# Earlier loads of x for batches 2 and 3, pooling ten chunks sooner, seven more softmax denominators on GpSimd, and a new order of the work

## The chip, the cores and the metric

The kernel runs on one core of a Trainium2 chip. Its metric is the device time of one execution in microseconds (us); lower is better. Nothing is exchanged with another core. Five engines work side by side and each runs its own list of instructions in the order in which the program put them: TensorE (PE in the profile, with PEld for its weight loads), VectorE (DVE), ScalarE (ACT), GpSimd (POOL) and SyncE (SP, which here only issues DMAs). An instruction that waits on a semaphore holds everything behind it on its engine.

## The reference

Two parts follow each other: an attention block with a few learned queries, and a feed-forward layer that takes the larger of two linear maps.

```python
B, N, m, C = 4, 12544, 32, 128
h = mab(I, x)            # 32 inducing points attend to all 12,544 rows of a batch ("pooling")
y = mab(x, h)            # each row attends to the 32 rows of h

def mab(q, kv):
    a = exp(scale * q @ kv.T - max);  a /= a.sum(-1) + 1e-09
    return a @ kv

h1, h2 = y @ w1, y @ w2                  # 128 -> 1024
out = maximum(h1, h2) @ w_out            # 1024 -> 128
```

Input and output are float32, 50,176 rows of 128 (25.7 MB each way).

## The kernel before, in words

A batch has 98 chunks of 128 rows. The maximum of two linear maps is computed as `h1 + relu(h2 - h1)`, and since every row of y is a mixture of the 32 rows of h, both maps are applied to h once for a batch (`hwd` for the difference w2 - w1, `m1` for w1 with w_out), so that the big matmuls contract over 32 values only. A chunk then passes these steps:

- **Scores** (`stage`, L596, L610; exp on ScalarE, L629): x transposed times h, four quarters of a block side by side in columns of the PE array ("column" mode). The result e2 (before division by its sum) is kept in six buffers.
- **Phases** (`phase`, L1011, matmuls L1069): four contractions over 32 rows run side by side in the four row groups of the array ("row" mode). Results go through relu to SBUF, by ScalarE (L1085) or VectorE (L1088).
- **Finals** (`final_one`, L864, L876): relu times w_out over eight pieces of 128, in the whole array ("full" mode).
- **Eviction** (`evict_group`, L893, L907): VectorE multiplies a group (mostly four chunks) by the reciprocal of the denominators and SP stores it (L935), from six output buffers.

The 28 blocks (7 a batch; blocks 0 to 6 are batch 0, 7 to 13 batch 1, 14 to 20 batch 2, 21 to 27 batch 3; block 20 is one chunk wide, most are four) have 108 groups.

The denominators of e2 come in one of two ways. `dens` (L656) has PE multiply e2 by ones (L671, one matmul for each chunk of width), VectorE takes the reciprocal from PSUM (L681). For a block marked `turned` (L594) SP transposes e2 by DMA (`den_turn`, L684, L688), GpSimd adds 32 values by halving in five additions (`den_sum`, L692, L698 and L700), and VectorE takes the reciprocal from SBUF (`den_rp`, L704, L707).

Pooling of batches 1 to 3 runs during the batch before: SP transposes x by DMA in 14 pieces (`transpose_x_dma`, L168, L172; batches alternate between two buffers), PE makes scores of 16 chunks at a time (`pool_scores`, L323, L329, six units), ScalarE the exp (L340), SP transposes it (`pool_turn`, L364, L366), and PE sums two units at a time with x (`pool_accum`, L369, L385). The transposed exps of the pooling and of the denominators share five buffers (tag `eT`). x itself is loaded by GpSimd's queue (`load_x`, L160, L166) into 12 buffers, seven for a batch. A one-element copy (`pace`, L164) ahead of the first load of a batch makes GpSimd wait for the value it reads. In the kernel before, the loads of batches 2 and 3 wait for the last pooling sum of the batch ahead (L418).

Batch 0 is different: its x is loaded first, transposed on PE (L235), copied from PSUM by VectorE (L246) or ScalarE (L249) as the table `COPY` says, and scored and summed in the order written in the string `HEAD`.

After the head a planner at build time sets the order. It keeps a clock of its own (`ck`) and at each step chooses between a phase, a final, scores and side work; the table `DEV` overrides it at numbered steps. Side work is put on a list at a count of finished chunks (L1103 to L1123) and issued once `ready` (L1129) says so by that clock. Which instruction waits for which is found afterwards, from the data.

Of the kernel before, what the change touches and what calls it, by code (L numbers as in the profile page):

```python
# [102 lines left out]
def kernel(  # L103
# [10 lines left out]
    B, N, C = x.shape  # L114
# [6 lines left out]
    P1 = 14  # L121
# [75 lines left out]
    with tc.manual_schedule(engines={ET.PE, ET.DVE, ET.Activation, ET.Pool, ET.SP}):  # L197
# [26 lines left out]
        st = [dict() for _ in range(B)]  # L224
# [90 lines left out]
        NU = K // U  # L315
# [48 lines left out]
        def pool_turn(b, u):  # L364
            eT = etp.tile([128, 4, 128], F16, name=f"eT_{b}_{u}", tag="eT", bufs=NEU)
            nc.sync.dma_start_transpose(eT, st[b]["eu", u][0].rearrange("p (j t) -> p j t", j=4))  # L366
            st[b]["eT", u] = eT, ck.pe

        def pool_accum(b, u):  # L369
# [52 lines left out]
            if last and b + 1 < B:  # L422
                for i in range(7):
                    load_x(b + 1, i, acc[:, C : C + 1] if i == 0 else None)
# [168 lines left out]
        for n, blk in enumerate(blocks):  # L593
            blk.turned = n > 20  # L594
# [128 lines left out]
        for n in ("h", "e"):  # L723
# [4 lines left out]
            ((0, 8, "A"), (8, 6, "D")),  # L728
            ((0, 6, "A"), (6, 8, "D")),
            ((0, 8, "A"), (8, 6, "D")),  # L730
            ((0, 6, "A"), (6, 8, "D")),
            ((0, 6, "A"), (6, 1, "A")),
            ((0, 5, "D"), (5, 2, "D")),
            ((0, 3, "D"), (3, 4, "A")),
            ((0, 4, "A"), (4, 3, "A")),
            ((0, 4, "D"), (4, 3, "D")),
            ((0, 4, "D"),),
            ((0, 2, "A"), (2, 1, "D")),
# [6 lines left out]
            T0.0 T0.1 C0.1 I C0.0 L0 T1.0 A0.2 C1.0 T1.1 C1.1 S0 S1 X0 X1 L1 H0 T2.0 E0 T2.1 C2.1 T3.0 C2.0  # L745
            A1.2 T3.1 S2 C3.0 X2 T4.0 H1 C3.1 L2 T4.1 S3 T5.0 T5.1 C4.0 H2 X3 C4.1 S4 T6.0 E1 C5.0 H3 T6.1
            X4 C6.0 C6.1 H4 T7.0 C5.1 E2 T7.1 S5 C7.0 T8.1 T8.0 C8.0 C8.1 C7.1 X5 S7 X7 S6 T9.0 H5 C9.0
            T10.0 T10.1 E5 X6 C10.0 C10.1 S8 E6 H7 X8 E4 N0.0 S10 S9 H6 E3 X9 H8 H9 E8 E9 E7 X10 E10 H10 e h
            W0.1 s N1.0 D0.1 G0 Y0.1 G1 Y1 D1.0 D2.1 Y0.2 W1.0 P0 w P1
# [143 lines left out]
        def evict_group(g, end):  # L893
# [38 lines left out]
            for b, c, s, m in runs:  # L932
                h = 2 if m == 4 and (groups.index(g) in (56, 60, 64, 68, 72, 76) or 78 <= groups.index(g) < 95) else m
# [26 lines left out]
        def want_linear():  # L960
# [142 lines left out]
        for b in range(1, B):  # L1103
            base = DONE0[b - 1]
# [24 lines left out]
        def ready(f, a):  # L1129

            now = ck.pe
            if f is den_turn:
                return a[0].staged <= now
            if f is den_sum:
                return a[0].den[1] + 7.5 <= now
# [184 lines left out]
```

## Time and profile before

| | |
|---|---|
| median of 3 runs | 324.26 us (324.13 to 324.92) |
| the profiled execution's own time | 324.39 us |
| its span, first to last instruction | 322.5 us |
| PE, DVE, ACT, POOL busy | 98%, 87%, 87%, 12% |
| granted PE clock | 1.0 throughout |
| PE's first and last matmul start | 1.19 and 319.43 us |

How to read it: the page gives busy time by engine, the span in 40 slices (tenths), the chain of work that ended last, and groups of instructions by source line with count, total and mean. A matmul's own duration overlaps the next one's, so the cost of a matmul is read from the distance between starts, or from the chain. About 1.9 us of the time lie outside the span.

### The profile page before, as it was taken

Reading aid. Unit: us, or ns where it says so; the run is one execution under the profiler, and the core shown is the slowest. Engines: PE = TensorE matmul, PEld = TensorE weight load, DVE = VectorE, ACT = ScalarE, POOL = GpSimd, SP = SyncE. Lnnn points to the kernel's source line nnn. Section 1 sums busy time; section 2 is a strip of 40 time slices with the busy share of each in tenths; the row PEclk is TensorE's granted clock in tenths of the full one; section 3 lists DMA queues with packets and bytes.
Section 4 is the critical chain, followed back from the end, with each engine's and each line's share of the span. In section 5 each row is a group of like instructions: output and inputs, shape, how many; then the busy total and the mean of one; then the engine's idle time right before and its main releaser. Section 6 shows DMA issues by size and latency. Waiting matters only on the chain.

```text
span 322.5 us, 12605 instructions
## 1 busy us (share of the span) xinstructions
PE 315.6 (98%) x5375; PEld 239.8 (74%) x5375; DVE 281.4 (87%) x508; ACT 281.8 (87%) x561; POOL 37.8 (12%) x90
## 2 busy tenths in 40 slices
PE   7899999999999999999999999999999999999996
PEld 3776777777777777777777777777777777777786
DVE  3369999988989998999989989988998999899974
ACT  3779999998978999999898999998869999999960
POOL 7470000000040000000040000000006400302000
PEclk9999999999999999999999999999999999999999
DMA  8999999954279999794279999893424322324233
GB/s 205 207 268 213 218 249 203 210 136 133 100 150 245 221 254 216 181 194 139 99 151 242 218 258 207 160 211 120 118 96 103 135 80 100 109 100 128 87 118 116
DMA packets 77320, 53.99 MB, mean 167 GB/s; under 512 B 56112, under 2 KB 64976, under 8 KB 77264
## 3 DMA queue, kind: packets, MB, share of 16 engines
q1 hardware_dynamic: 71232, 39.42, 50.0%
q0 software_dynamic: 5888, 13.70, 21.7%
q8 instruction: 42, 0.69, 0.9%
q14 instruction: 14, 0.11, 0.1%
q10 hardware_dynamic: 144, 0.07, 0.1%
HBM read 27.28 MB, written 25.69 MB: 164 GB/s over the span
## 4 chain that ended last, share of the span: by engine, by line
PE 93%; DMA 5%; ACT 1%; issue 1%; POOL 0%; DVE 0%; POOLq 0%
PE ps L876 62%; PE ps L1069 22%; DMA xn<-in_x_dram 5%; PE ps L610 2%; PE ps L385 2%; PE ps L329 1%; PE ps L671 1%; PE ps L833 1%; ACT e L629 0%; PE ps L505 0%; ACT hwd L482 0%; PE ps L235 0%; PE ps L303 0%; PE ps L430 0%; PE ps L258 0%
## 5 line engine op out<-in xcount | busy, mean ns | idle before, releaser
L1085 ACT ACTIVATE relu<-ps 128x512 f16<-128x512 f32 x462 | 244.1, 604 | 23.0 <-PE ps L1069 15.0
L1088 DVE TENSOR_SCALAR relu<-ps 128x512 f16<-128x512 f32 x322 | 206.1, 682 | 16.2 <-PE ps L1069 14.8
L876 PE MATMUL ps<-woutp,relu 128*128 128x128 f16 x3136 | 216.9, 220 | 0.0
L876 PEld LDWEIGHTS <-relu 128*128 128x128 f16 x3136 | 176.6, 98 | 39.4 <-issue 28.9
L1069 PE MATMUL ps<-e,hwd 32*128 32x512 f16 (+2 forms) x888 | 88.2, 358 | 0.1
L907 DVE TENSOR_TENSOR o<-ps,rp 128x512 f32<-128x512 f32 (+3 forms) x80 | 51.2, 640 | 1.8 <-PE ps L876 1.3
L1069 PEld LDWEIGHTS <-hwd 32*128 32x128 f16 x888 | 24.5, 91 | 20.9 <-issue 0.8
L1069 PE MATMUL ps<-m,e 32*128 32x128 f16 x381 | 38.7, 217 | 0.0
L1069 PEld LDWEIGHTS <-e 32*128 32x128 f16 x381 | 21.2, 92 | 2.9 <-issue 0.4
L907 DVE TENSOR_TENSOR o<-ps,rpt 128x512 f32<-128x512 f32 (+3 forms) x28 | 17.3, 618 | 4.1 <-PE ps L853 2.2
L166 POOL DMA_DIRECT2D xn<-in_x_dram x33 | 17.8, 553 | 6.7 <-DMA xn<-in_x_dram 4.6
L164 POOL COPY pace<-hacc 128x1 f32<-128x1 f32 x2 | 0.4, 188 | 133.1 <-DVE hacc L418 133.1
L246 DVE COPY xT<-ps 128x768 f16<-128x768 f16 (+6 forms) x11 | 4.8, 458 | 8.9 <-PE ps L235 8.9
L340 ACT ACTIVATE eu<-ps 128x512 f16<-128x512 f32 x18 | 10.9, 614 | 0.1
L629 ACT ACTIVATE e<-ps 128x512 f16<-128x512 f32 (+2 forms) x21 | 10.4, 568 | 0.2 <-PE ps L610 0.2
L235 PE MATMUL ps<-identity,xn 128*128 128x128 f16 x98 | 8.1, 219 | 2.3 <-DMA xn<-in_x_dram 1.8
L535 POOL COPY m1bd<-m 32x128 f16<-32x128 f16 x4 | 1.1, 287 | 76.7 <-DVE m L530 76.6
L249 ACT COPY xT<-ps 128x768 f16<-128x768 f16 (+5 forms) x10 | 6.5, 671 | 3.0 <-PE ps L235 2.9
L698 POOL TENSOR_TENSOR w1T<-den 128x256 f32<-128x256 f16 (+1 forms) x7 | 4.4, 633 | 38.6 <-DMA den<-e 38.6
L700 POOL TENSOR_TENSOR w1T<-w1T 128x64 f32<-128x64 f32 (+4 forms) x28 | 8.4, 302 | 2.2
L235 PEld LDWEIGHTS <-xn 128*128 128x128 f16 x98 | 5.6, 97 | 4.0 <-DMA xn<-in_x_dram 2.2
L610 PE MATMUL ps<-xT,hT 128*32 128x512 f16 (+3 forms) x114 | 8.2, 361 | 0.0
(93 smaller groups left out, 117.0 us busy)
## 6 DMA issues: line engine op xcount, KB each, us to landing
out_dram<-o SPq DMA_DIRECT2D x68, 256.0 KB, 2.8
xn<-in_x_dram POOLq DMA_DIRECT2D x24, 448.0 KB, 10.1
out_dram<-o SPq DMA_DIRECT2D x54, 128.0 KB, 1.8
wf<-in_moe_w_dram POOLq DMA_DIRECT2D x4, 256.0 KB, 5.9
xn<-in_x_dram POOLq DMA_DIRECT2D x3, 224.0 KB, 8.8
xT<-xn SPq DMA_TRANSPOSE x42, 3.8
xf<-in_x_dram SPq DMA_DIRECT2D x1, 512.0 KB, 3.7
xf<-in_x_dram SPq DMA_DIRECT2D x1, 384.0 KB, 4.2
```

The source lines that it names most:

```text
L166: nc.gpsimd.dma_start(out=xn_at[b, i][lo:hi, 0:n, :], in_=xr[b, lo:hi, k0 : k0 + n, :])
L235: nc.tensor.transpose(ps[:, j, :], xn_at[0, i][:, g + j, :], identity16)
L249: nc.scalar.copy(out=dst, in_=ps[:, 0:m, :])
L340: nc.scalar.activation(out=eu, in_=ps, func=AF.Exp, scale=scale, accum_out=st[b]["es"][:, u : u + 1])
L610: nc.tensor.matmul(out=ps[32 * q : 32 * (q + 1), 128 * t : 128 * (t + n)], lhsT=hq, rhs=xT[:, c : c + n, :], start=True, stop=True, tile_p ...
L629: nc.scalar.activation(out=blk.e2[:, lo:hi], in_=ps[:, lo:hi], func=AF.Exp, scale=st[0]["rs"] if blk.b == 0 else scale,)
L700: nc.gpsimd.tensor_add(acc[:, :, 0:n], acc[:, :, 0:n], acc[:, :, n : 2 * n])
L876: nc.tensor.matmul(out=g.ps[:, 128 * c : 128 * (c + 1)], lhsT=g.blk.relu[q][:, 128 * (jb * w4 + t) : 128 * (jb * w4 + t + 1)], rhs=woutp[: ...
L907: nc.vector.tensor_mul(osb[:, 0:n, :], g.ps[:, 0 : n * C].rearrange("p (s c) -> p s c", s=n), rp)
L1069: nc.tensor.matmul(**seq[i])
L1085: nc.scalar.activation(out=dst, in_=src, func=AF.Relu)
L1088: nc.vector.tensor_scalar(out=dst, in0=src, scalar1=0.0, scalar2=None, op0=ALU.max)
```

## The change

- `load_x` of batches 2 and 3 moves from the end of `pool_accum` to the end of `pool_turn` of the last unit; the first load now waits for the last pooling exp of the batch ahead.
- Pooling of batches 2 and 3 (x transposes, scores, transposes of the exps, sums) is put on the list 10 chunks earlier.
- Blocks 9, 10, 11, 12, 16, 19 and 20 become `turned`: their denominators go by DMA transpose and GpSimd. Outside the last batch GpSimd's additions are released 4.0 us (not 7.5) after the transpose by the planner's clock.
- In the head, `COPY` hands other pieces to the other engine, and `HEAD` has a new order: among others the first cast of w1 by GpSimd stands ahead of the first load of batch 1's x, and the subtraction w2 - w1 is made in four pieces of 256 rather than two of 512.
- Seven groups (88 to 94) are no longer stored in halves.
- `DEV` is new from step 948 on.

```diff
@@ pool_turn
             st[b]["eT", u] = eT, ck.pe
+            if u == NU - 1 and b + 1 < B:
+                for i in range(7):
+                    load_x(b + 1, i, st[b]["eu", u][0][:, 0:1] if i == 0 else None)
@@ pool_accum
-            if last and b + 1 < B:
-                for i in range(7):
-                    load_x(b + 1, i, acc[:, C : C + 1] if i == 0 else None)
@@
-            blk.turned = n > 20
+            blk.turned = n > 18 or n in (9, 10, 11, 12, 16)
@@ COPY
-            ((0, 8, "A"), (8, 6, "D")),
+            ((0, 8, "D"), (8, 6, "A")),
             ((0, 6, "A"), (6, 8, "D")),
-            ((0, 8, "A"), (8, 6, "D")),
+            ((0, 7, "A"), (7, 7, "A")),
             ((0, 6, "A"), (6, 8, "D")),
-            ((0, 6, "A"), (6, 1, "A")),
-            ((0, 5, "D"), (5, 2, "D")),
-            ((0, 3, "D"), (3, 4, "A")),
-            ((0, 4, "A"), (4, 3, "A")),
-            ((0, 4, "D"), (4, 3, "D")),
+            ((0, 7, "D"),),
+            ((0, 7, "D"),),
+            ((0, 2, "D"), (2, 5, "A")),
+            ((0, 4, "D"), (4, 3, "A")),
+            ((0, 7, "D"),),
             ((0, 4, "D"),),
-            ((0, 2, "A"), (2, 1, "D")),
+            ((0, 2, "D"), (2, 1, "A")),
@@ HEAD (the last two lines of each)
-            T10.0 T10.1 E5 X6 C10.0 C10.1 S8 E6 H7 X8 E4 N0.0 S10 S9 H6 E3 X9 H8 H9 E8 E9 E7 X10 E10 H10 e h
-            W0.1 s N1.0 D0.1 G0 Y0.1 G1 Y1 D1.0 D2.1 Y0.2 W1.0 P0 w P1
+            H7 N3.0 E6 S9 E4 S10 E3 H8 X10 N2.0 X9 E8 H6 E10 E7 E9 e H9 H10 W0.1 h s D0.1 N5.0 N4.0 G0 G1
+            Y0.1 Y1 Y0.2 D1.0 D2.1 W1.0 P0 w P1
@@ evict_group
-                h = 2 if m == 4 and (groups.index(g) in (56, 60, 64, 68, 72, 76) or 78 <= groups.index(g) < 95) else m
+                h = 2 if m == 4 and (groups.index(g) in (56, 60, 64, 68, 72, 76) or 78 <= groups.index(g) < 88) else m
@@ DEV
...
@@ when side work is listed
-            base = DONE0[b - 1]
+            base = DONE0[b - 1] - (10 if b > 1 else 0)
@@ ready
             if f is den_turn:
-                return a[0].staged <= now
+                d = st[a[0].b + 1] if a[0].b < B - 1 else {}
+                quiet = a[0].b == B - 1 or a[0].index >= 7 or ("T", 13) in d and ("eT", NU - 1) in d
+                return a[0].staged <= now and quiet
             if f is den_sum:
-                return a[0].den[1] + 7.5 <= now
+                return a[0].den[1] + (7.5 if a[0].b == B - 1 else 4.0) <= now
```

More of the change, by code (lines that the diff above doesn't have):

```diff
@@ L727 @@
         COPY = (
-            ((0, 8, "A"), (8, 6, "D")),
+            ((0, 8, "D"), (8, 6, "A")),
             ((0, 6, "A"), (6, 8, "D")),
-            ((0, 8, "A"), (8, 6, "D")),
+            ((0, 7, "A"), (7, 7, "A")),
             ((0, 6, "A"), (6, 8, "D")),
-            ((0, 6, "A"), (6, 1, "A")),
-            ((0, 5, "D"), (5, 2, "D")),
-            ((0, 3, "D"), (3, 4, "A")),
-            ((0, 4, "A"), (4, 3, "A")),
-            ((0, 4, "D"), (4, 3, "D")),
+            ((0, 7, "D"),),
[3 more added lines that the diff above has]
+            ((0, 7, "D"),),
             ((0, 4, "D"),),
-            ((0, 2, "A"), (2, 1, "D")),
+            ((0, 2, "D"), (2, 1, "A")),
         )
         HEAD = """
-            T0.0 T0.1 C0.1 I C0.0 L0 T1.0 A0.2 C1.0 T1.1 C1.1 S0 S1 X0 X1 L1 H0 T2.0 E0 T2.1 C2.1 T3.0 C2.0
-            A1.2 T3.1 S2 C3.0 X2 T4.0 H1 C3.1 L2 T4.1 S3 T5.0 T5.1 C4.0 H2 X3 C4.1 S4 T6.0 E1 C5.0 H3 T6.1
-            X4 C6.0 C6.1 H4 T7.0 C5.1 E2 T7.1 S5 C7.0 T8.1 T8.0 C8.0 C8.1 C7.1 X5 S7 X7 S6 T9.0 H5 C9.0
-            T10.0 T10.1 E5 X6 C10.0 C10.1 S8 E6 H7 X8 E4 N0.0 S10 S9 H6 E3 X9 H8 H9 E8 E9 E7 X10 E10 H10 e h
-            W0.1 s N1.0 D0.1 G0 Y0.1 G1 Y1 D1.0 D2.1 Y0.2 W1.0 P0 w P1
+            T0.0 T0.1 C0.0 C0.1 I A0.2 L0 T1.0 T1.1 C1.0 C1.1 S0 S1 X0 X1 L1 H0 E0 T2.0 T2.1 C2.1 T3.0 C2.0
+            T3.1 S2 C3.0 H1 C3.1 X2 T4.0 S3 A1.2 X3 T5.0 C4.0 H2 H3 L2 S4 T6.1 X4 T6.0 C6.1 C5.0 E1 H4 T7.0
+            S5 C6.0 E2 T7.1 T8.0 C7.0 C8.0 C7.1 X5 S7 X7 S6 X6 T9.0 H5 T10.1 T10.0 C9.0 C10.0 C10.1 S8 E5 X8
+            H7 N3.0 E6 S9 E4 S10 E3 H8 X10 N2.0 X9 E8 H6 E10 E7 E9 e H9 H10 W0.1 h s D0.1 N5.0 N4.0 G0 G1
+            Y0.1 Y1 Y0.2 D1.0 D2.1 W1.0 P0 w P1
         """
```

22 rows, old and new, of the table DEV are left out of this document.

## The prediction

> **What bounds the kernel now.** I read the page first (busy shares, clock, the chain of work that ended last), then busy time by stretch, then the chain in order of time.
>
> ```profile
> PE 315.6 (98%) x5375; PEld 239.8 (74%) x5375; DVE 281.4 (87%) x508; ACT 281.8 (87%) x561; POOL 37.8 (12%) x90
> PEclk9999999999999999999999999999999999999999
> PE 93%; DMA 5%; ACT 1%; issue 1%; POOL 0%; DVE 0%; POOLq 0%
> ```
>
> ```profile
> 30.00:90.00 60.00, 60.00 (x1050) 45.28 (x1047) 56.14 (x97) 55.42 (x114) 0.11 (x1) 1.00 0.82 180
> 90.00:150.00 60.00, 60.00 (x1010) 44.69 (x1007) 55.12 (x96) 55.39 (x114) 3.80 (x8) 1.00 0.95 206
> 150.00:210.00 60.00, 60.00 (x1008) 45.59 (x997) 56.05 (x99) 55.04 (x108) 3.89 (x8) 1.00 0.87 185
> 210.00:270.00 60.00, 60.00 (x1044) 45.95 (x1040) 54.39 (x99) 54.31 (x110) 8.68 (x24) 1.00 0.47 124
> 270.00:318.00 48.00, 48.00 (x809) 38.08 (x808) 42.32 (x74) 40.41 (x78) 5.20 (x15) 1.00 0.31 103
> ```
>
> The columns of the second fence are the stretch, its length, and busy time of PE, PEld, DVE, ACT and POOL, then clock, DMA share, GB/s. The reader is to see 60.00 of 60.00 for PE: from 30 us to 318 us TensorE never stands still, at the full clock, while VectorE and ScalarE are at about 92%. A busy PE need not be PE at its best, so I also looked at the distance between matmul starts, and they are regular throughout.
>
> ```profile
> by line: PE ps L876 61.8%; PE ps L1069 22.4%; DMA xn<-in_x_dram 4.6%; PE ps L610 2.1%; PE ps L385 1.5%; PE ps L329 1.5%; PE ps L671 0.6%; issue 0.6%; PE ps L833 0.5%; ACT e L629 0.4%; PE ps L505 0.4%; ACT hwd L482 0.3%; PE ps L235 0.3%; PE
> 10.04 7.70 DMA xn<-in_x_dram
> 31.97 0.94 PE ps L876 x15
> 33.24 0.83 PE ps L876 x13
> 91.94 0.33 PE ps L1069 x4
> 92.43 0.43 PE ps L505 x2
> 103.68 0.18 PE ps L671 x8
> ```
>
> These are lines of the chain (start, us, what). Two finals more cost 0.11 us, so a final costs 0.055, and a run of 13 costs 0.83 - 13 x 0.055 = 0.11 more than its matmuls: that is the turn of the array from full to row mode. The other way, a 512-wide matmul costs 0.43 / 2 = 0.215, and four of them side by side in row mode take 0.33 until the finals go on: again 0.11 more, of which I count 0.10 as the turn, since these times are read to 0.01 and rounded both ways. So after the head there is only one currency: what the program makes PE do. Work taken from PE shortens the time one for one, a wait put on PE lengthens it one for one, and all the rest costs nothing as long as it makes PE wait for nothing.
>
> **The change part by part: PE's work.** Comparing the two programs' lists of PE instructions, everything has the same count but L671: 76 matmuls before, 51 after. The seven blocks that leave are six of four chunks and one of one chunk, 25 matmuls. The chain gives L671 0.6% of 322.5 us, 1.94 us for 76, or 0.0255 each (8 in a row: 0.18, which agrees). Saving: 25 x 0.0255 = **0.64 us**. The same lists give the turns between the array's modes: 478 before, 473 after (full to row 220 to 222, row to full 204 to 203, column to full 24 to 23, row to column 19 to 20, full to column 8 to 4, column to row 3 to 1). Five turns at 0.10 are **0.5 us**. Nothing else of the new order changes PE's own work. Sum 1.14 us.
>
> **What takes over the denominators.**
>
> ```profile
> L671 PE MATMUL ps<-ones_q,e 128*128 128x4 f16 x76 | 3.5, 165 | 0.1
> L681 DVE RECIPROCAL rp<-ps 128x32 f32<-128x32 f32 (+3 forms) x11 | 3.5, 320 | 0.0
> L707 DVE RECIPROCAL rpt<-w1T 128x16 f32<-128x16 f32 (+1 forms) x7 | 1.6, 235 | 0.0
> L698 POOL TENSOR_TENSOR w1T<-den 128x256 f32<-128x256 f16 (+1 forms) x7 | 4.4, 633 | 38.6 <-DMA den<-e 38.6
> L700 POOL TENSOR_TENSOR w1T<-w1T 128x64 f32<-128x64 f32 (+4 forms) x28 | 8.4, 302 | 2.2
> ```
>
> GpSimd gets seven times one addition at 0.633 and four at 0.302: 1.84 us each, 12.9 in all, on an engine that is 12% busy. VectorE does three reciprocals from PSUM less (11 to 8) and seven from SBUF more: 7 x 0.235 - 3 x 0.320 = 0.7 us over 200 us, beside the 8% it has free. The danger is order, not length: a reciprocal in VectorE's list that waits for GpSimd holds the relu behind it, and then PE's PSUM banks. In the new lists at least 12 groups are stored between the transpose of such a block outside the last batch and its first eviction (7 in the last batch); at 290 us / 108 groups = 2.7 us a group that is 32 us (19 us) for a chain of at most 10.6 (the latest landing below) + 1.84. Cost zero; without that cover, a held VectorE would cost PE the wait less a bank or two.
>
> SP gets seven more DMA transposes and seven store issues fewer (groups 88 to 94 whole). A transpose takes 1.23 to 1.29 of its issue time, a store 0.33 to 0.53 (rows below): +8.8, -2.8 us, on a queue that is off the path. Fewer halves delay nothing that ends the kernel: those groups are far from the last, and the six output buffers cover 6 x 2.7 = 16 us.
>
> **The loads.**
>
> ```profile
> 71.52 0.62 ACT L340 ACTIVATE eu<-ps 128x512 f16<-128x512 f32 x1
> 89.89 0.19 POOL L164 COPY pace<-hacc 128x1 f32<-128x1 f32 x1 [65.84 <-DVE hacc L418]
> 90.38 3.72 POOL L166 DMA_DIRECT2D xn<-in_x_dram  x7 [0.30 <-PE ps L876]
> ```
>
> The last pooling exp of batch 1 ends at 72.1, so its wait is over 18 us before the old one. Five of the seven loads start at about 72.5; the last two take the place of the first 28 chunks of batch 1 and wait for the sum that reads them, near 78. The transposes of batch 2 come 10 chunks (some 8 us) sooner, so their loads gain 10 us on them. For batch 3 the last exp itself comes sooner. The direct worth for PE is nil, as no wait for x is in the chain after 18 us. What it does move is the stretch in which the DMA engines are full:
>
> ```profile
> 72.00:92.00 20.00, 20.00 (x406) 15.76 (x402) 18.87 (x38) 16.36 (x33) 1.81 (x5) 1.00 0.37 110
> 92.00:112.00 20.00, 20.00 (x326) 14.57 (x322) 18.07 (x32) 18.01 (x35) 2.10 (x4) 1.00 1.07 220
> ```
>
> ```profile
> 77.98 2.19 SPq L366 DMA_TRANSPOSE eT<-eu  x1
> 102.61 1.23 SPq L172 DMA_TRANSPOSE xT<-xn  x1
> 103.94 1.62 SPq L935 DMA_DIRECT2D out_dram<-o  x1
> 105.62 5.92 SPq L172 DMA_TRANSPOSE xT<-xn  x1
> 112.26 1.23 SPq L172 DMA_TRANSPOSE xT<-xn  x1
> 87.85 0.63 PE L385 MATMUL ps<-xn,eT 128*32 128x128 f16 x32
> ```
>
> ```profile
> eT<-eu SPq DMA_TRANSPOSE x1, 3.3
> out_dram<-o SPq DMA_DIRECT2D x1, 256.0 KB, 8.7
> xT<-xn SPq DMA_TRANSPOSE x1, 10.6
> out_dram<-o SPq DMA_DIRECT2D x1, 128.0 KB, 9.6
> xT<-xn SPq DMA_TRANSPOSE x1, 8.8
> ```
>
> The last fence is DMA issues with us from issue to landing, for 77 to 80 us (first line), 102 to 103.5 and 105 to 106. While the loads run (92 to 112 us, DMA share 1.07), all of SP's queue lands late: 8.7 to 10.6 us, and one transpose held the queue for 5.92. The changed loads run at about 72 to 94, and in there stands the transpose of batch 1's last exp, issued at 77.98. It landed in 3.3; PE reads it in the second half of the sum that starts at 87.85, at about 88.1, so it has 10.1 us. With the loaded landings of 8.7 to 10.6, PE waits between 0 and 0.5 us. If a 5.92 us hold comes ahead of it, the wait is up to 5.92 + 10.6 - 10.1 = 6.4. I take 0, since three of the four loaded landings fit and this transpose is the smaller (4 tiles against 7), and keep 0 and 6.4 as ends.
>
> A page of the Trainium skill bears on this: "DMA: Bandwidth & Descriptors", section "Queues, rings and completion order", has each DMA engine serve its queues in turn, a packet at a time. By that a transpose's delay should go with its packets, 10.6 x 4/7 = 6.1 us, and PE would not wait at all. The stores in the rows speak for a delay that does not shrink with size (128 KB took 9.6, 256 KB 8.7); by them the wait is the 0 to 0.5 above. The sum is the same to 0.5 us.
>
> **The head.** Up to 18 us it follows the arrival of x (the chain's 7.70 us of DMA), which is unchanged. After that:
>
> ```profile
> 19.32 0.37 ACT L249 COPY xT<-ps 128x256 f16<-128x256 f16 x1
> 19.67 0.94 ACT L274 ACTIVATE et<-ps 128x224 f16<-128x224 f32 x3
> 20.27 0.69 DVE L779 TENSOR_TENSOR w<-wf 128x512 f16<-128x512 f32 x1 [0.66 <-DMA wf<-in_moe_w_dram]
> 21.03 0.29 DVE L451 TENSOR_SCALAR hT<-ps 128x128 f16<-128x128 f32 x1
> ```
>
> ScalarE's copy ahead of the last three exps becomes one of 128 instead of 256 columns, about 0.1 less. Against it, the subtraction of 0.69 waits for the weights until 20.27 and becomes two of half the width before hT; a fixed part is paid twice, an estimated 0.1 to 0.2 in all, and the first now ends at or after the 21.03 at which hT started. I take 0 for the head, with ends -0.25 (only the shorter exps count) and +0.25 (only the subtractions count).
>
> **Sum.** Profiled execution 324.39 - 0.64 - 0.5 = 323.25. That execution lies 0.13 above the median of the runs, 324.26, from which the same steps give 323.12. I predict **323.2 us**, 0.33% faster; 0.3% (1 us) is about what a measurement of this kernel can tell from no change. Own range 322.8 to 323.6: the head's bounds and 0 to 0.3 of the wait.
>
> **The rivals.**
>
> *More than PE's own work is gained.* The head ends sooner by its bound and the turns are worth 0.11 each: 324.26 - 1.19 - 0.25 = 322.8, and to 322.5 if the head has more in it than I see. Against it: PE has no other idle time to give after 30 us (60.00 of 60.00).
>
> *It does not do what it says: the gain is taken back by small waits.* In the stretch of batch 2's 14 transposes of x, SP issues 20 transposes and 13 stores: 20 x 1.29 + 13 x 0.53 = 32.7 us, in 13 groups of 2.7 = 35 us. Before it was 16 and 12: 27.0 in 32. The queue is nearly full; a hold of 5.92 puts it 3.6 us behind, and pooling scores come late. PE then waits 0.3 to 2 us: 323.6 to 325.2. For it: the 5.92 row. Against it: the same hold, with less slack than 5.92, made PE wait for nothing before, and the earlier loads should be through before these transposes start.
>
> *Slower.* The transpose of batch 1's last exp is late at the PE sum near 88 us, and PE, whose list is in order, stands. The landing decides: beyond 88.1 + 1.14 = 89.2 the gain is gone, beyond 90.2 (12.2 us after issue) it is slower by over 0.3%. The loaded landings seen end at 10.6, so it takes a hold of the queue as well. Price up to 6.4 us: 325.3 to 329.6.
>
> **How the numbers follow.** Forecast 0.56 (of it 0.40 under 323.29, the 0.3% bound, and 0.16 over it), more gained 0.08, taken back 0.18, slower 0.18. Faster 0.40 + 0.08 = 0.48; the same 0.16 + 0.18 = 0.34; slower 0.18. The range 322.5 to 325.2 leaves out the slower case and a little of the best.
>
> **What would show it.** Right: PE still 60.00 of 60.00 in each stretch from 30 to 270 us; 51 matmuls at L671; the last PE start about 1.1 us earlier; reciprocals at L707 with no idle time ahead of them; loads at about 72 us with the full DMA stretch moved there. The slower case would show as PE idle just ahead of the pooling sum near 88 us, behind a DMA; the third as waits of PE at pooling scores between 110 and 210 us. I am wrong altogether if PE waits for relu (VectorE or ScalarE held in the new order), which neither list can show.

## The result: 10.7 us slower

| | median of runs | range | ratio to before |
|---|---|---|---|
| before | 324.26 us | 324.13 to 324.92 | |
| changed kernel | 334.99 us | 333.81 to 335.33 | 1.032 (1.0299 to 1.0342) |

The forecast was 323.2 us with a range up to 325.2. The profiled execution of the changed kernel took 335.01 us, its span 333.2 us. The lines of its page that answer to those shown of before (busy time, PE's slices and granted clock, the chain of work that ended last):

```profile
PE 316.3 (95%) x5350; PEld 240.7 (72%) x5350; DVE 281.6 (84%) x513; ACT 280.4 (84%) x559; POOL 50.8 (15%) x125
PE   7899999999549999999999999999999999999994
PEclk9999999999959999999999999999999999999999
PE 87%; DMA 10%; ACT 1%; issue 1%; POOL 0%; DVE 0%; POOLq 0%; ACTq 0%
```

PE is busy as long as before (316.3 against 315.6 us), in a span that is 10.7 us longer. Its slices have one hole, a 5 and a 4 at 83 to 100 us, and the granted clock has a 5 in the second of them. The chain's share of DMA has gone from 5% to 10%. Busy time by stretch (columns as in the prediction):

```profile
30.00:90.00 60.00, 57.61 (x979) 43.26 (x977) 55.36 (x95) 54.75 (x112) 3.91 (x8) 1.00 1.08 195
90.00:150.00 60.00, 53.93 (x887) 40.17 (x891) 45.56 (x82) 46.15 (x95) 7.61 (x20) 0.91 0.82 177
150.00:210.00 60.00, 60.00 (x1015) 45.61 (x1011) 55.34 (x100) 56.10 (x112) 7.74 (x18) 1.00 1.05 189
```

All idle time of PE behind the head lies around 90 us; from 150 us on it is 60.00 of 60.00 again. PE's part of the timeline there (start, us, what, and in brackets the idle time ahead and what ended it), with SP's and GpSimd's issues a little earlier, and the DMA issues of SP at 73.8 and 77.7 us and of GpSimd's last load, at 78.4 us, with their us to landing:

```profile
91.45 0.62 PE L388 MATMUL ps<-xn,eT 128*32 128x128 f16 x16 [3.84 <-DMA eT<-eu]
96.69 0.62 PE L388 MATMUL ps<-xn,eT 128*32 128x128 f16 x16 [4.62 <-DMA eT<-eu]
```

```profile
73.81 1.70 SPq L366 DMA_TRANSPOSE eT<-eu  x1
77.67 5.89 SPq L366 DMA_TRANSPOSE eT<-eu  x1
72.47 2.67 POOL L166 DMA_DIRECT2D xn<-in_x_dram  x5 [0.30 <-PE ps L1069]
77.87 1.11 POOL L166 DMA_DIRECT2D xn<-in_x_dram  x2 [2.73 <-PE ps L388]
```

```profile
eT<-eu SPq DMA_TRANSPOSE x1, 17.6
eT<-eu SPq DMA_TRANSPOSE x1, 19.0
xn<-in_x_dram POOLq DMA_DIRECT2D x1, 448.0 KB, 17.3
```

The loads start when the forecast said. The transposes of batch 1's last two exps fall among them: the first, at 73.81 us, while the first five loads are being issued, the second, at 77.67, behind these five and 0.2 us ahead of the last two. They land after 17.6 and 19.0 us, so at 91.4 and 96.7; before they took 2.4 and 3.3. The last load lands at 95.7. PE reads both transposed exps in the last pooling sum of batch 1, and waits for each.

Against tight starts of the same matmuls (each start less what the matmuls and turns ahead of it must take by the prices of the prediction), PE's account is an estimate: own work -1.1 us, head -0.3, the two waits +3.9 and +4.9, the half clock between 90 and 100 us +1.4, some 0.6 in small pieces. So the last matmul starts 9.3 us later (328.76 against 319.43), and the end behind it is 1.4 us longer (4.5 against 3.1): the last stores are issued as soon as before but land later, for which I have no cause.

### The profile page after: what moved, and what is told of

Its sections match the earlier page's. It is cut to its first block, busy times and chain, and to the rows that moved or that the text cites. A ratio compares the mean times of both kernels' runs of the same rounds, so it can differ in the third digit from the quotient of the medians.

```text
span 333.2 us, 12600 instructions
## 1 busy us (share of the span) xinstructions
PE 316.3 (95%) x5350; PEld 240.7 (72%) x5350; DVE 281.6 (84%) x513; ACT 280.4 (84%) x559; POOL 50.8 (15%) x125
## 4 chain that ended last, share of the span: by engine, by line
PE 87%; DMA 10%; ACT 1%; issue 1%; POOL 0%; DVE 0%; POOLq 0%; ACTq 0%
PE ps L876 58%; PE ps L1069 21%; DMA eT<-eu 6%; DMA xn<-in_x_dram 4%; PE ps L610 2%; PE ps L329 1%; PE ps L388 1%; PE ps L833 0%; ACT e L629 0%; PE ps L505 0%; PE ps L671 0%; ACT hwd L482 0%; PE ps L235 0%; PE ps L430 0%; PE ps L303 0%
## 5 line engine op out<-in xcount | busy, mean ns | idle before, releaser
L1085 ACT ACTIVATE relu<-ps 128x512 f16<-128x512 f32 x462 | 243.9, 604 | 34.0 <-PE ps L1069 14.8
L907 DVE TENSOR_TENSOR o<-ps,rpt 128x512 f32<-128x512 f32 (+3 forms) x54 | 34.2, 634 | 5.6 <-PE ps L876 2.9
L907 DVE TENSOR_TENSOR o<-ps,rp 128x512 f32<-128x512 f32 (+3 forms) x54 | 34.2, 633 | 0.6 <-PE ps L876 0.2
L698 POOL TENSOR_TENSOR w1T<-den 128x256 f32<-128x256 f16 (+2 forms) x14 | 8.7, 622 | 141.3 <-DMA den<-e 115.8
L700 POOL TENSOR_TENSOR w1T<-w1T 128x32 f32<-128x32 f32 (+5 forms) x56 | 16.7, 298 | 4.4
L388 PE MATMUL ps<-xn,eT 128*32 128x128 f16 x288 | 6.1, 230 | 8.5 <-DMA eT<-eu 8.5
L388 PEld LDWEIGHTS <-eT 128*32 128x32 f16 x288 | 4.5, 100 | 10.3 <-DMA eT<-eu 9.0
L246 DVE COPY xT<-ps 128x1024 f16<-128x1024 f16 (+3 forms) x10 | 5.3, 538 | 7.9 <-PE ps L235 7.9
L421 DVE TENSOR_TENSOR hacc<-ps,hacc 128x128 f32<-128x128 f32 (+1 forms) x6 | 1.8, 293 | 9.5 <-PE ps L407 8.4
```

The source lines that it names most:

```text
L388: nc.tensor.matmul(out=ps[32 * g : 32 * (g + 1), 0:128], lhsT=eT[:, j, 32 * g : 32 * (g + 1)], rhs=xn_of(b, U * v + 4 * g + j), start=(j = ...
L698: nc.gpsimd.tensor_add(acc, eT[:, :, 0 : M // 2], eT[:, :, M // 2 : M])
L700: nc.gpsimd.tensor_add(acc[:, :, 0:n], acc[:, :, 0:n], acc[:, :, n : 2 * n])
L907: nc.vector.tensor_mul(osb[:, 0:n, :], g.ps[:, 0 : n * C].rearrange("p (s c) -> p s c", s=n), rp)
L1085: nc.scalar.activation(out=dst, in_=src, func=AF.Relu)
```

## The experiments

All ratios are to the kernel before, run on the same chip, with 95% intervals.

**1. The loads alone, in the kernel before.**

```diff
             st[b]["eT", u] = eT, ck.pe
+            if u == NU - 1 and b + 1 < B:
+                for i in range(7):
+                    load_x(b + 1, i, st[b]["eu", u][0][:, 0:1] if i == 0 else None)
...
-            if last and b + 1 < B:
-                for i in range(7):
-                    load_x(b + 1, i, acc[:, C : C + 1] if i == 0 else None)
```

> The kernel before with only the loads of x moved behind the last pooling exp. Theory: the whole loss and none of the gain, 324.3 + 8.5 of waits + 1.7 of clock = 334.5 us (333 to 336). Rival (the loads harm only together with the new order and the added transposes): 324.3 us.

Measured: 333.36 us (332.77 to 333.82), ratio 1.0275 (1.0259 to 1.0291). Here only the last exp's transpose (issued at 77.87 us, in 1.24) falls among the loads, the last of which lands at 95.0; its landing, and PE's wait:

```profile
eT<-eu SPq DMA_TRANSPOSE x1, 17.4
```

```profile
95.27 0.62 PE L388 MATMUL ps<-xn,eT 128*32 128x128 f16 x16 [7.13 <-DMA eT<-eu]
```

The loads alone make the loss, in the place that the theory names. With one transpose among the loads instead of two PE still waits 7.1 us, since the later one decides when the sum can end.

**2. Everything but the loads.**

```diff
             st[b]["eT", u] = eT, ck.pe
-            if u == NU - 1 and b + 1 < B:
-                for i in range(7):
-                    load_x(b + 1, i, st[b]["eu", u][0][:, 0:1] if i == 0 else None)
...
+            if last and b + 1 < B:
+                for i in range(7):
+                    load_x(b + 1, i, acc[:, C : C + 1] if i == 0 else None)
```

> The changed kernel with the loads of x back at the end of the last pooling sum; all else of the change stays. Theory (the loads, issued ahead of the transposes of batch 1's last two exps, make these land late, PE stands 3.8 + 4.6 us for them near 88 and 92 us and then runs 10 us at half its clock): no wait of PE at the last pooling sum of batch 1, time 323.1 us (322.8 to 323.6), the 1.1 us of PE's own work kept. Rival (SP's fuller queue or the new order is what makes the transposes late): still 330 us or more, with the wait in place.

Measured: 335.92 us (335.64 to 337.53), ratio 1.0366 (1.0345 to 1.0386). The theory fell: the wait at the pooling sum is gone, and others of the same size are in its place. The longest, as SP, VectorE and PE show it in the timeline:

```profile
95.23 1.31 SPq L172 DMA_TRANSPOSE xT<-xn  x1
96.66 0.51 SPq L935 DMA_DIRECT2D out_dram<-o  x1
97.26 10.25 SPq L688 DMA_TRANSPOSE den<-e  x2
111.93 0.69 DVE L907 TENSOR_TENSOR o<-ps,rp 128x512 f32<-128x512 f32 x1 [5.39 <-DMA out_dram<-o]
112.67 0.26 PE L1069 MATMUL ps<-m,e 32*128 32x128 f16 x1 [4.61 <-DVE o L907]
```

The us to landing of SP's first transpose and of its first store in that list:

```profile
xT<-xn SPq DMA_TRANSPOSE x1, 16.3
out_dram<-o SPq DMA_DIRECT2D x1, 128.0 KB, 15.1
```

From the bottom: PE waits for a PSUM bank, since VectorE has not evicted. VectorE waits for an output buffer, since a store has not landed: the sixth eviction back is that of the store of 96.66, which lands at 111.8, just ahead of VectorE's 111.93. That store (its eviction ended at 92.2) stood on SP behind a transpose of x, which waited for its x until 95.2 and lands at 111.5; the last of the seven loads (now from 90.15 us on) lands at 111.2. In the kernel before five stores in a row among the loads had no transpose ahead of them, and landed after 8.0 to 10.3 (the 8.7 of the prediction is one). The two transposes of new denominators held the queue for 10.25 us (before, a transpose with no load in flight was issued in 1.2 to 2.5), but the store that VectorE waited for had been issued ahead of them, so that hold did not make this wait. "On a queue that is off the path" and six buffers that "cover 6 x 2.7 = 16 us" are wrong too, as soon as the loads no longer hide it.

**3. The loads behind the last transposed exp**, so that nothing of batch 1's pooling stands behind them:

```diff
-                    load_x(b + 1, i, st[b]["eu", u][0][:, 0:1] if i == 0 else None)
+                    load_x(b + 1, i, eT[:, 0, 0:1] if i == 0 else None)
```

> The changed kernel, but the first load of batches 2 and 3 waits until the transpose of the last exp has landed (the pacing copy reads the transposed exp instead of the exp). Loads then start near 81.5 us, 9 us later than in the changed kernel and 9 sooner than before. Theory: no wait of PE, 323.1 us. Rival (any load in that stretch slows the pooling sum or the stores enough to hold PE): 326 us or more.

Measured: 327.59 us (327.02 to 328.83), ratio 1.0101 (1.0083 to 1.0118). The waits at the pooling sum are gone, which settles their cause. What is left sits at 133 us (SP, GpSimd, VectorE and PE in the timeline):

```profile
95.73 8.08 SPq L688 DMA_TRANSPOSE den<-e  x2
130.81 1.48 POOL L700 TENSOR_TENSOR w1T<-w1T 128x128 f32<-128x128 f32 x4
132.32 0.25 DVE L707 RECIPROCAL rpt<-w1T 128x16 f32<-128x16 f32 x1 [2.68 <-POOL w1T L700]
133.17 0.39 PE L1069 MATMUL ps<-e,hwd 32*128 32x512 f16 x2 [1.70 <-DVE relu L1088]
```

SP, held for 8.08 us at 96, goes from one issue to the next without a gap until 140 us. The transposes of blocks 11 and 12 come out at 125.3 and 126.6 us, GpSimd's sums end at 132.3, VectorE's reciprocal waits for that, the relu behind the reciprocal is late, and PE stands: the danger that the forecast named ("order, not length") and put at zero.

The reciprocal that waits is the second of batch 1's four (the first is at 116.22), and GpSimd had made the first two sums by 111.0; it waits for the fourth. `den_sum` puts the sums into two halves of one buffer in turn (L695), and the planner lets later sums go ahead of an earlier block's reciprocal. So the 12 groups of cover, which the forecast counted from a block's own transpose to its own eviction, say nothing of this wait. By the code and this order three sums stand in two halves when it ends, so one block is divided by the sums of another; the kernel before has the same order in batch 3.

**4. Five loads behind the exp, the last two of batch 2 behind the last pooling sum.**

```diff
-                for i in range(7):
+                for i in range(5 if b == 1 else 7):
...
+            if last and b == 1:
+                for i in range(5, 7):
+                    load_x(b + 1, i, acc[:, C : C + 1] if i == 5 else None)
```

> The changed kernel with five of batch 2's seven loads behind the exp and the last two behind the last pooling sum. If a transpose lands when the loads issued ahead of it are through (five of them at about 90 us), both transposes land near 91.5: PE waits 3.8 us once and not a second time, and its clock falls later or not, 327 to 328 us. If instead the second transpose is late because it held SP's queue for 5.9 us or because of a fixed delay under load, the second wait of 4.6 us stays: 332 us or more.

Measured: 329.01 us, one run. PE waits 1.9 and 1.4 us for the two transposes, so both expectations miss: the second wait shrinks with the first, and neither goes. With two loads behind the exp and five later:

> The changed kernel with two loads of batch 2 behind the last exp and five at the end of the last pooling sum (with five and two: 329.01 us, landings of 16.0 and 13.5 us). Theory (transposes land some 2 us after the loads issued ahead): the two loads are through by 80 us, the transposes land 3 to 8 us after issue and PE doesn't wait for them; the five loads from 90 us on meet the sooner pooling, with waits near 112 us or later: 325 to 333 us. Rival (any load ahead makes them late): the transposes land 12 us or more after issue.

Measured: 328.07 us, one run; no wait at the pooling sum, 2.9 us in all at 134 us. Landings of the two transposes (issued at about 73 to 74 and 78 us), first with five loads ahead, then with two:

```profile
eT<-eu SPq DMA_TRANSPOSE x1, 16.0
eT<-eu SPq DMA_TRANSPOSE x1, 13.5
```

```profile
eT<-eu SPq DMA_TRANSPOSE x1, 10.8
eT<-eu SPq DMA_TRANSPOSE x1, 8.0
```

For the second transpose that is 3.3, 8.0, 13.5 and 19.0 us with no load, two, five and seven in the burst: some 2.2 us a load. What decides is not how many loads were issued ahead. With five, the first transpose was issued at 73.84 us between the second load and the third (73.93), and lands at 89.8 all the same; the fifth load lands at 90.0, the second transpose at 91.6. With two loads the burst is through at 83.6, and the transposes land at 84.0 and 85.8. So a transpose lands about when the loads that share its time are through. The theory's 3 to 8 us for two loads was too low, and its "loads issued ahead" should be the whole burst.

**5. Half the bytes in the same seven loads.**

```diff
-            nc.gpsimd.dma_start(out=xn_at[b, i][lo:hi, 0:n, :], in_=xr[b, lo:hi, k0 : k0 + n, :])
+            m = n // 2 if b == 2 else n
+            nc.gpsimd.dma_start(out=xn_at[b, i][lo:hi, 0:m, :], in_=xr[b, lo:hi, k0 : k0 + m, :])
```

> The changed kernel, but the seven loads of batch 2 bring only the first half of their rows (so half of what is computed for batch 2 uses older rows); their count, order and issue stay. Theory (the transposes starve until the bytes of the loads issued ahead are through, 16 us for seven full ones): they are through by some 81 us, both transposes land by 84 us, PE waits nowhere: 323.2 us (322.9 to 324.5). Rival (the count of loads, or their issue, makes the lateness): the transposes still land 14 us or more after issue, 330 us or more.

Measured: 325.54 us (324.05 to 330.43), ratio 1.0021 (1.0004 to 1.0038) without the three longest. Seven executions took 324.05 to 326.32 us, three 329.8 to 330.4, and the profile is of the longest; against 17.6 and 19.0 its landings are

```profile
eT<-eu SPq DMA_TRANSPOSE x1, 10.7
eT<-eu SPq DMA_TRANSPOSE x1, 13.1
```

Count and issue of the loads are the same, the lateness is not: it goes with what the loads move, though not in proportion. Here the last load lands at 90.6 us and the second transpose at 90.9; the theory's 84 for both was too early, and PE waits 2.9 us. In the seven shorter executions, of which there is no profile, the times leave room for little or no wait. The rival, a fixed lateness for any seven loads, fell.

**6. Keeping PE busy in the two waits.** Dummy matmuls stand ahead of each. They write into the bank of the pooling sum and change what is computed for batch 1.

```diff
             for v in (u - 1, u):
+                if last and b == 1:
+                    for _ in range(36 if v < u else 46):
+                        nc.tensor.matmul(
+                            out=ps[:, 256:512], lhsT=warm[:, 0:128], rhs=warm[:, 0:256],
+                            start=True, stop=True, skip_group_check=True,
+                        )
```

> The changed kernel with 36 and 46 matmuls of 256 columns by a constant tile (into columns that nothing reads) ahead of the two waits for the transposed exps of batch 1. The two waits stay as long as they are, but PE isn't idle in them. Theory: some 1.5 us of the loss is the half clock behind the waits: 333.4 us (332.8 to 334.0), full clock granted from 90 to 101 us. Rival: the half clock costs nothing by itself, or is granted whatever PE does: 334.9 us or more.

Measured: 332.88 us (332.51 to 333.11), ratio 1.0264 (1.0247 to 1.0281): 2.1 us less than the changed kernel. The clock row of its page, and the dummies in the timeline:

```profile
PEclk9799999999999999999999999999999999999999
```

```profile
88.23 4.10 PE L386 MATMUL ps<-warm 128*128 128x256 f16 x36
92.60 5.20 PE L386 MATMUL ps<-warm 128*128 128x256 f16 x46
```

From the third slice on the full clock is granted, although PE does nothing useful for longer (9.3 us) than it waited. So the half clock is a part of the loss by itself. Start by start against the changed kernel, the same matmuls come 0.69 us later here up to the two sums (a longer head in this execution), 0.71 later at the first final behind them, and 0.55 earlier from 103.6 us to the end: the full clock is worth 1.3 us. The rest of the 2.1 is the end behind the last matmul (3.1 against 4.5 us), less the longer head.

**7. Each other part by itself.** First the pooling ten chunks sooner, in the kernel before:

```diff
-            base = DONE0[b - 1]
+            base = DONE0[b - 1] - (10 if b > 1 else 0)
```

> The kernel before with one line of the change alone: the pooling of batches 2 and 3 put on the list ten chunks sooner; loads, denominators and order as before. Theory (SP's transposes of x, issued while the seven loads are in flight, hold SP, and the stores behind them are late): output buffers run out near 112 us as in the run with the old denominators (337.41 us), 333 to 338 us. Rival (the new order or the new denominators are what meets the loads): no wait, 323.9 to 324.6 us.

Measured: 331.10 us (330.80 to 331.97), ratio 1.0218 (1.0204 to 1.0232), 2 us less than the theory's range. The wait is where the theory had it. SP's transposes of x between 94 and 112 us (min/median/max of their issue in ns), while the loads are in flight:

```profile
L172 SPq DMA_TRANSPOSE xT<-xn x3: 1320/3838/10287, 95.1 to 108.0; - x3
```

VectorE waits 5.3 us for a store at 111.81, PE 4.5 us for VectorE at 112.56. The chain of late store, full output buffers and late eviction is that of experiment 2: the store was issued at 96.54 us behind the first of these transposes (95.11) and landed after 15.2, at 111.7. The transpose that held SP for 10.3 us was issued behind that store. In the kernel before the first transpose of x came at 102.61, behind five stores among the loads.

Then the new set of turned blocks alone, in the kernel before:

```diff
-            blk.turned = n > 20
+            blk.turned = n > 18 or n in (9, 10, 11, 12, 16)
```

> The kernel before with the larger set of turned blocks alone (51 matmuls by ones instead of 76; its order of PE isn't fitted to it and has 0.8 us more of its own work, by the distances between starts). Theory: the two transposes of denominators near 95 us are held on SP behind the loads, the stores behind them are late, and PE waits by 112 us: 328 to 333 us. Rival (they fit in): 325.1 us (324.7 to 325.6).

Measured: 329.58 us (329.41 to 330.43), ratio 1.0172 (1.0156 to 1.0187). Waits of its trace (total us, times, longest):

```profile
DVE o L907 <- DMA out_dram<-o: 2.0, 1, 2.0
PE ps L1069 <- DVE o L907: 1.6, 1, 1.6
```

PE waits where the theory said (1.6 us at 113.5), but not by the hold that it named: the two new transposes of 95 us were issued in 3.1 us, and the store behind them, at 98.17, landed after 14.5. The wait is less than half of the 5.3 us; by starts some 0.8 is PE's own work in an order not fitted to it, some 1.8 us are spread from 130 to 220 us, where PE is busy for 89.94 of 90.00 us by its records, and the rest I have not traced.

And the head alone (`COPY` and `HEAD` of the changed kernel in the kernel before):

> The kernel before with the changed order of the head (the tables COPY and HEAD) alone. Theory, by the starts in the two traces: 0.3 us sooner, 323.95 us (323.8 to 324.1). Rival, the forecast's: nothing, 324.0 to 324.5 us.

Measured: 324.13 us (323.96 to 325.03), ratio 1.0000 (0.9991 to 1.0009). Nothing, as forecast.

**8. Which part is needed for the waits in experiments 2 and 3.** With the old denominators in both (`blk.turned = n > 20`):

> As the run with the loads back at the end of the last pooling sum (335.92 us), but with the denominators of the kernel before. Theory: SP's 10.3 us in two transposes of denominators, in the middle of seven loads, is what ran the output buffers out; without them 323.5 to 324.5 us. Rival: pooling ten chunks sooner is what puts transposes and stores into the loads: 328 us or more.

Measured: 337.41 us (335.85 to 337.60), ratio 1.0397 (1.0373 to 1.0420). The theory fell: without the transposes of denominators, those of x take their place on SP. PE waits 4.3 us at 112.55, for a store of 96.70 behind a transpose of x, and 2.3 at a pooling score of batch 3 for a transpose of x.

> As the run with the loads behind the last transposed exp (327.59 us), but with the denominators of the kernel before (only blocks 21 to 27 turned, 76 matmuls by ones). Theory: the waits of that run are the price of the four new turned blocks of batch 1 on SP; without them none is left, and PE's own work is 0.3 us more than with them: 323.5 us (323.1 to 324.2). Rival: the loads alone hold SP and some wait stays: above 325 us.

Measured: 325.76 us (324.94 to 326.44), ratio 1.0047 (1.0029 to 1.0066). The wait for GpSimd is gone, so the new denominators make it, as the theory had it; but 0.5 us of wait for a transpose of x is left at 133, and the time is in the rival's range. With the old delay between a block's transpose and its sum in experiment 3 (`7.5` for `4.0`):

> As the run with the loads behind the last transposed exp (327.59 us), but GpSimd's sums are put 7.5 us behind a block's transpose again instead of 4.0. Theory: the 2.7 us that PE lost near 133 us there came from VectorE's reciprocal (L707) put too soon behind a sum, whose transpose SP had issued some 6 us late; with 3.5 us more between them the wait goes, with it the 3.4 us at half clock: 323.2 us (322.8 to 324.0). Rival: SP's backlog is what counts and the wait comes back at the same block's eviction: 326 to 328 us.

Measured: 327.93 us (325.93 to 330.49), ratio 1.0119 (1.0066 to 1.0173). The rival holds: the reciprocal still waits 2.2 us for GpSimd, so SP's lateness counts and not the planned distance. With the old time of the pooling in experiment 2 (`base = DONE0[b - 1]`):

> The changed kernel with the loads back at the end of the last pooling sum and the pooling at its old count of chunks; the new denominators and the order stay. Theory A (only the sooner pooling meets the loads): no wait left, 323.3 to 324.0 us. Theory B (any transpose on SP behind the loads is held, those of blocks 9 and 10 at some 96 us too): SP held 8 to 10 us there, and a wait of PE stays: 326 to 333 us.

Measured: 331.39 us (330.33 to 332.46), ratio 1.0211 (1.0195 to 1.0227). Theory B holds for the wait, not for the hold: PE waits 2.1 us at 113.66 and 2.2 at 189.83, both for output buffers whose stores, issued behind transposes of denominators, landed after 14.8 and 15.2 us. SP's issue of the two transposes there took 3.3 us, not 8 to 10. And the old time of the pooling in experiment 3:

> As the run with the loads behind the last transposed exp (327.59 us), with the pooling at its old count of chunks. Theory: the loads are through by 98 us, before the first transpose of x for batch 2, so SP has no backlog, VectorE's reciprocal finds its sum ready, and the forecast's PE work comes out: 323.2 us (322.9 to 324.0). Rival: the two transposes of denominators at 95 us alone make the backlog: 326 us or more.

Measured: 324.61 us (324.43 to 324.93), ratio 1.0011 (1.0002 to 1.0020). Its first two stretches, and SP's issue of the new denominators and of the first transpose of x:

```profile
30.00:90.00 60.00, 60.00 (x1047) 45.23 (x1044) 56.15 (x97) 55.37 (x114) 3.91 (x8) 1.00 0.98 190
90.00:150.00 60.00, 59.95 (x976) 44.58 (x975) 54.01 (x97) 54.71 (x113) 7.59 (x20) 1.00 0.98 203
```

```profile
95.13 3.81 SPq L688 DMA_TRANSPOSE den<-e  x2
103.00 1.28 SPq L172 DMA_TRANSPOSE xT<-xn  x1
```

This is the only version with the new denominators in which PE loses next to nothing: the loads are issued at 81.9 to 85.0 us, behind the pooling's last transposes, and the last lands at 104.0, so that of SP's transposes only those of the denominators and the first of x meet them. (The expectation had the loads through by 98.) Yet it is not faster. PE's own work is 0.73 us less by tight starts (the 0.64 of L671, but only one turn of the array saved, 477 against 478), but the last matmul starts only 0.15 us earlier (319.29 against 319.43), as 0.75 us come back in small waits (0.3 of it from 90 to 100 us, 0.3 from 160 to 170) and the head gives 0.2; and the end behind it is 0.5 us longer. The last stores are not the reason:

```diff
-                h = 2 if m == 4 and (groups.index(g) in (56, 60, 64, 68, 72, 76) or 78 <= groups.index(g) < 88) else m
+                h = 2 if m == 4 and (groups.index(g) in (56, 60, 64, 68, 72, 76) or 78 <= groups.index(g) < 95) else m
```

> As the run with the loads behind the last transposed exp and the pooling at its old count (324.61 us), with the stores of groups 88 to 94 halved again as in the kernel before. Theory: SP's last stores end 0.5 us later without it (320.45 against 319.97 us in the two profiles); with it 324.2 us (323.9 to 324.4). Rival: the end hangs on something else, 324.6 us.

Measured: 324.90 us (324.55 to 326.03), ratio 1.0020 (1.0011 to 1.0029). The theory fell, the rival holds. Why the end is 0.5 us longer stays open. No version that I ran beats the kernel before.

The runs side by side (us):

| loads of x | pooling | denominators | time |
|---|---|---|---|
| behind the last exp | sooner | new | 334.99 (the change) |
| behind the last exp | old | old | 333.36 in the old order |
| behind the last transposed exp | sooner | new | 327.59 |
| behind the last transposed exp | sooner | old | 325.76 |
| behind the last transposed exp | old | new | 324.61 |
| behind the last sum | sooner | new | 335.92 |
| behind the last sum | sooner | old | 337.41, and 331.10 in the old order |
| behind the last sum | old | new | 331.39, and 329.58 in the old order |
| behind the last sum | old | old | 324.26 in the old order (before) |

## Why the prediction was wrong

**PE's own work: right as far as the runs tell.** These are two groups of the changed kernel's view by line (count, busy time, mean ns of one, and idle time ahead):

```profile
L671 PE MATMUL ps<-ones_q,e 128*128 128x4 f16 x51 | 2.4, 165 | 0.1
L707 DVE RECIPROCAL rpt<-w1T 128x16 f32<-128x16 f32 (+2 forms) x14 | 3.3, 235 | 0.0
```

51 matmuls at L671, and the 1.14 us less by tight starts is the forecast's own sum over the program of PE; no run shows it in a time. From 150 to 270 us PE is at 60.00 of 60.00, and the reciprocals at L707 have no idle time ahead, as announced.

**The loads: the step that failed.** It reads: "With the loaded landings of 8.7 to 10.6, PE waits between 0 and 0.5 us", with "I take 0". Three things were wrong in it.

- The size. The rows of 8.7 to 10.6 us were for issues at 102 to 106 us, late in their burst: of its loads (from 90.38 on) three had landed by 102.61, and the last lands at 112.4. The transpose of 102.61 lands at 113.2, so its 10.6 us was the rest of the burst. The transposes of the change were issued 1.3 and 5.2 us after the first load, before any had landed (the first does at 78.4, the last at 95.7), and the rest of the burst was 17.6 and 19.0 us. The row was the nearest by kind, but not by what was still to come. Landings go with the burst's length (experiment 4) and its bytes (5).
- The count. The forecast looked at one transpose. Two fell among the loads, and PE reads them one after the other, so it waited twice.
- The end of the range. The 6.4 added a hold of the queue to a loaded landing. The two waits came to 8.8 us, without the hold deciding: the transpose that waited longest took 5.89 us of issue, but in experiment 1 it took 1.24 and landed after 17.4 all the same. And a waiting PE drops to half the clock, 1.3 us more by experiment 6 and 1.4 by tight starts, which no row of before could show, as PE never stood there.

The slower rival named the engine, the place and the cause, and gave 325.3 to 329.6 with a chance of 0.18. The time lies 5.4 us above its end: 2.4 of wait beyond its 6.4, the clock, the longer end of 1.4, and small pieces.

The Trainium skill, "DMA: Bandwidth & Descriptors", section "Queues, rings and completion order", lets each DMA engine take its queues in turn, packet by packet, from which the prediction had an estimate of 6.1 us. The traces don't agree with it as a measure of delay: 17.6 and 19.0 us, growing with the loads in flight on the other queue.

**SP and the denominators: a second step that failed, hidden by the first.** "On a queue that is off the path" and "Cost zero" hold only in the changed kernel, where PE's wait at 90 us gives everything behind it 9 us. Without that wait a transpose comes on SP while the loads are in flight, lands only at their end, and the stores behind it land just after it, some 15 us after their issue and up to 20 after the eviction: that uses up the 16 us of output buffers (experiments 2, 7 and 8). A held issue did not make these waits, since each of these stores was issued ahead of the held transpose. The rival "taken back by small waits" saw the full queue (32.7 of 35 us) but priced its waits at 0.3 to 2 us; they are up to 4.6 us each. In experiment 3 what remains is another part of the same step: the order of sums and reciprocals.

**Why batch 3 cost nothing.** Its loads were moved in the same way. In the changed kernel's trace (SP's issue, its landing, PE's sum):

```profile
152.14 1.24 SPq L366 DMA_TRANSPOSE eT<-eu  x1
```

```profile
eT<-eu SPq DMA_TRANSPOSE x1, 12.4
```

```profile
165.83 0.63 PE L388 MATMUL ps<-xn,eT 128*32 128x128 f16 x32
```

One transpose, issued just ahead of the first load (152.23) instead of among them, and read at about 166: it had 14 us and took 12.4. That was luck of 1.6 us; 0.1 us ahead of the loads it was still five times slower than the 2.5 of before.

**The head: right**, nothing within what a measurement tells.

**The order of the costs.** The parts don't add: loads alone +9.1, sooner pooling alone +6.9, denominators alone +5.3, all together +10.7. As far as the traces show they share one cause: transposes on SP meet seven loads in flight. Whichever meets them first delays PE, and so gives the others their time.

## What to carry to other kernels

When a burst of loads is moved, list what other DMAs are issued from its start until its last load has landed, and give each transpose a landing at the burst's end, whatever its own size; a row measured late in a burst says nothing of its beginning. Then look at the stores behind such a transpose on the same queue: they land behind it, and the output buffers have to cover that. And before a cost is set to zero because it is hidden, ask what hides it, since a wait that goes uncovers the next one.

## What the runs showed of the hardware

**The half clock comes by stretches of 3.4 us, decided by the one before.** Busy time of PE (the third number) and granted clock (ahead of the DMA share), in neighbouring stretches of 3.4 us: first of the kernel of experiment 3, then of the version with the old delay, then of the one with two loads behind the exp, then of experiment 2, with stretches laid where the clock records put them.

```profile
130.90:134.30 3.40, 1.50 (x13) 0.50 (x11) 1.98 (x5) 1.80 (x4) 1.15 (x4) 1.00 0.82 135
134.30:137.70 3.40, 3.40 (x59) 2.48 (x57) 2.18 (x5) 1.28 (x3) 0.00 (x0) 0.50 0.99 222
```

```profile
130.30:133.70 3.40, 1.99 (x22) 1.00 (x20) 1.83 (x4) 2.39 (x5) 1.24 (x4) 1.00 0.78 109
133.70:137.20 3.50, 3.50 (x59) 2.59 (x60) 2.34 (x5) 1.23 (x4) 0.00 (x0) 0.51 0.99 229
```

```profile
129.60:133.00 3.40, 2.45 (x38) 1.84 (x37) 0.62 (x2) 3.08 (x6) 2.85 (x9) 1.00 0.99 186
133.00:136.40 3.40, 2.20 (x47) 1.39 (x50) 3.25 (x7) 0.84 (x2) 0.12 (x1) 1.00 0.78 177
```

```profile
136.60:140.00 3.40, 2.25 (x27) 1.15 (x24) 2.82 (x6) 1.72 (x4) 0.46 (x2) 1.00 0.60 154
140.00:143.40 3.40, 3.40 (x58) 2.13 (x53) 1.80 (x4) 2.35 (x6) 0.00 (x0) 0.50 0.95 212
```

By starts PE lost 2.7 and 2.2 us in the first two, and a stretch at half the clock followed. It lost 2.9 us in the third and none followed, because the loss fell across two stretches: PE was busy 1.50 and 1.99 of 3.4 us in the first two, 2.45 and 2.20 in the third. Busy time alone does not draw the line: in the fourth PE was busy for 2.25 us, and half the clock followed. Over all traces here a stretch at the full clock with PE busy for 1.83 us or less was always followed by one at half, and one with 2.34 or more never; between 2.0 and 2.3 both came, and what decides there is not shown. The Trainium skill, "TensorE: Matmul & The Clock Gate", section "What's actually happening", has a window of 3.4 us that runs on by itself; with that the traces agree. The same page of the Trainium skill, section "Why this matters for your kernels", asks for no gap of over some 3 us; here 2.2 us was enough.

**A DMA transpose issued while the loads are in flight lands about when they are through**, though the two come from different queues. With two, five and seven loads of 448 KB the second transpose came after 8.0, 13.5 and 19.0 us (3.3 without loads), 2.2, 1.6 and 0.9 us behind the last load. It is no exact rule: with half the bytes the first transpose landed at 84.2 us, 3.6 ahead of the fifth load, and the transpose of batch 3 that was issued 0.1 us ahead of its loads landed at 164.5, with the second of them (164.9). **A store behind such a transpose on SP's queue landed after some 15 us** (15.1 in experiment 2), 0.3 us behind the transpose; with no transpose ahead, the five stores of the kernel before landed after 8.0 to 10.3.

**The issue of a DMA transpose can hold its queue while loads are in flight**: up to 10.3 us (the L172 row of experiment 7), against 1.2 to 2.5 in the kernel before with none. Not every one is held: the first of that row took 1.32 us, that of experiment 1 took 1.24. What decides is not shown.
